# Two channel-mix pieces beside each of modes 51 to 60, and the early identity passes ahead of mode 61

## The chip, the cores and the metric

The kernel runs on one core of one Trainium2 chip. The metric is the device time of one launch in microseconds, as the median of several executions. Times inside an execution come from a hardware profile of one of them and count from its first instruction. PE is the matmul engine (TensorE), PEld its weight loads, DVE is VectorE, ACT ScalarE, POOL GpSimd and SP SyncE.

## The reference

The work is an attention layer followed by a spectral mixing layer, for batch 8, sequence 576, width 512 (8 heads of 64).

```
attn_out = attention(q, k, v)        # heads 0-3 local mask, heads 4-7 strided mask
x  = attn_out as (8, 576, 512)
X  = rfft(x, axis=1)                 # only modes 0..63 are used
Yr = Xr[m] @ w_r[m] - Xi[m] @ w_i[m] # per mode m, 512x512 weights
Yi = Xr[m] @ w_i[m] + Xi[m] @ w_r[m]
y  = irfft(Y, n=576)
u  = x + y
out = u + relu(u @ w_ch)             # the channel mix
```

The weights `w_r` and `w_i` are 64 matrices of 512 x 512 each in float32, read once. They make most of the traffic.

## The kernel before

The order of all work is written out by hand; each engine runs its own instructions in the order in which the program names them and waits on semaphores for the others.

**Stages.** First the strided heads of all batches, then the local heads together with the modes of "slot 0" (one half of the 512 input rows of every weight matrix), then the modes of "slot 1" (the other half) together with the channel mix of x, and last the tail that makes the output rows. The change lies in slot 1 and at its end.

**Weights.** `w_fetch` (L180) issues two DMAs on GpSimd's queue for a mode, 256 KB each as written into SBUF in float16: 64 rows of `w_r` and of `w_i`. There are 12 weight buffers. Every call of `mode` issues one later fetch, so the fetches are written down about twelve modes ahead of their use. The same buffers later hold the tail's `rl` and `osb`.

**Modes.** `mode(slot, m)` (L504) makes 16 matmuls with 16 columns each (L515) into a PSUM bank `y` that eight modes share. At the last mode of a bank DVE adds the result to slot 0's share (L543, `YT`). For the last bank there are two such adds: after mode 61 for modes 56 to 61, and after mode 63 for the last two.

**Pieces beside the modes of slot 1.** The list `work` has 76 pieces: four `w_turn`, and for each of the eight batches four `turn` and five `premix`.

- `turn` (L550) transposes attention results on PE into a PSUM tile `tp` (L559 six transposes, L580 five); DVE copies them out as `xT` in two copies (L565 and L571, or L585 and L589).
- `premix` (L599) multiplies a row block of `xT` by the channel weights, four matmuls of 512 columns into PSUM `sc` (L613), and transposes the block back into `tp`, four transposes (L621). ACT copies `sc` to `v0` or `v0h` (L622), DVE copies `tp` to `xo` or `xoh` (L623). The last block of a batch (t = 4) has 64 rows.
- `spec` (L801) follows certain modes, not by the list: after modes 52 and 56 among others. It transposes finished spectra `YT` into `tp` (L632) and multiplies them by the channel weights (L635); ACT makes four copies `zz` (L641), DVE four copies `yy` (L642).

Two `tp` buffers, two `sc` and two `av` exist in this stage, and two banks for `y`. After the pieces their pools are closed and the banks go to new pools `v` and `u`, three buffers each.

**End of slot 1 and tail.** `v_early` (L854) and `u_early` (L873) put `v0` and `xo` of the first three output blocks into the new banks with one identity matmul of 512 columns each: six early identity passes. Then mode 63 runs. `spec_last` (L846, L844) handles the last 16 modes, and for each of 36 output blocks `v_rows` (L648, L651) and `u_rows` (L663, L666) add the inverse transform, ACT applies relu (L865), GpSimd or PE adds x, DVE adds the two (L884), and SP or ACT's queue writes the block out.

The lines that set the end of slot 1:

```
for i in range(3):
    v_early(i)
    u_early(i)
mode(1, NM - 1)
spec_last(0)
spec_out(3, 0, *held[0])
```

Of the kernel before, what the change touches and what calls it, by code (L numbers as in the profile page):

```python
# [19 lines left out]
NM = 64  # L20
# [57 lines left out]
def kernel(  # L78
# [27 lines left out]
    def psum(kind, half=False):  # L106
        if half:
            return pss[kind].tile([128, 1024], F16, tag=kind, name=kind)
        return pss[kind].tile([128, 512], FP, tag=kind, name=kind)
# [27 lines left out]
    def spectra_tile(n):  # L137
        if n == "X0":
            Xh[0] = big.tile([128, 4, B, 2, NM], F16, tag=n, name=n)
        else:  # L140
            YS[n] = big.tile([128, 4, 4, 16, 16], F16, tag=n, name=n)
# [23 lines left out]
    def w_fetch(n=1):  # L165
        for _ in range(n):
            i = len(w_tiles)
            if i >= 2 * NM:
                return
            half, m = 1 - i // NM, i % NM  # L170
            if i in GUEST:
                n, j = GUEST[i]
                if j == 0:
                    guests[n] = big.tile([128, 2, 4, DM], F16, tag=n, name="wt")
                wt = guests[n][:, j]
            else:
                wt = pw.tile([128, 4, DM], F16, tag="w", name="wt")

            for ri, src in enumerate([moe_w_r, moe_w_i] if m else [moe_w_r]):
                nc.gpsimd.dma_start(  # L180
                    wt[ds(64 * ri, 64)],
                    src[m, ds(256 * half, 256), :].rearrange("(p c) e -> p c e", c=4),
                )
            w_tiles.append(wt)
# [284 lines left out]
    def dft(b, half):  # L469
        if half == 0 and b == 0:  # L470
            spectra_tile("X0")
        xp = psum("sc" if half else "y")
        tiles = (
            [(t, (JG[t % 3][1] - JG[t % 3][0]) * NCB) for t in range(6)]
            if half
            else [(t, SCS[t]) for t in range(5)]
        )
        F = cs["cFs"] if half else cs["cFl"]
        base = 0 if half else 6
        for cp in range(2):  # L480
            for i, (t, n) in enumerate(tiles):
                nc.tensor.matmul(  # L482
                    xp[:, ds(192 * cp, 192)],
                    xb[b][0:n, base + t, ds(128 * cp, 128)],
                    F[0:n, t, :],
                    start=(i == 0),
                    stop=(i == len(tiles) - 1),
                )
        xv = xp[:, 0:384].rearrange("p (c x) -> p c x", c=2)
        X = Xh[half]  # L490
        for src in range(2):
            for dst in range(2):
                args = dict(
                    out=X[ds(64 * dst, 64), ds(2 * src, 2), b].rearrange(
                        "p c g m -> p c (g m)"
                    ),
                    in_=xv[ds(64 * src, 64), :, ds(64 - 64 * dst, 128)],
                )
                act_copy(**args)
# [4 lines left out]
    def mode(slot, m):  # L504
        half = 1 - slot
        mi, mg = m % 8, m // 8
        if mi == 0:
            ypt[slot] = psum("y")
        yp = ypt[slot]
        yv = yp.rearrange("p (m e x) -> p m e x", m=8, e=4)  # L510
        wt = w_tiles[slot * NM + m]
        pr = ds(0, 128 if m else 64)
        for e in range(4):
            for c in range(4):
                nc.tensor.matmul(  # L515
                    yv[:, mi, e, :],
                    wt[pr, XC[c], ds(128 * e, 128)],
                    Xh[half][pr, c, :, :, m],
                    start=(c == 0),
                    stop=(c == 3),  # L520
                )
        if slot or m not in GUEST:
            w_fetch()
        ends = {7: 8}
        if slot and mg == 7:
            ends = {5: 6, 7: 2}
        if mi in ends:
            n = ends[mi]
            m0 = mi + 1 - n
            part = (  # L530
                slice(None),
                slice(None),
                mg // 2,
                slice(None),
                ds(8 * (mg % 2) + m0, n),
            )
            src = yp.rearrange("p (m e x) -> p e x m", m=8, e=4)[:, :, :, ds(m0, n)]
            if slot == 0:
                if m == 7:
                    spectra_tile("Y0")  # L540
                nc.scalar.activation(out=YS["Y0"][part], in_=src, func=ACTF.Copy)
            else:
                nc.vector.tensor_tensor(  # L543
                    out=YS["YT"][part], in0=src, in1=YS["Y0"][part], op=AluOp.add
                )
# [138 lines left out]
    def str_front(b):  # L684
        return [
            lambda: str_v(b, 0), lambda: str_v(b, 1),
            lambda: str_v(b, 2), lambda: str_q(b, 0),
            lambda: str_back(b, 0),
            lambda: str_back(b, 1), lambda: str_q(b, 1),
            lambda: str_k(b, 0),  # L690
            lambda: str_k(b, 1), lambda: str_k(b, 2),
        ]
# [12 lines left out]
    first = str_front(0)  # L705
# [38 lines left out]
    for b in range(B):  # L744
# [5 lines left out]
        work = [  # L750
            scores[0], front[0], scores[1], ends[0], front[1], values[0], front[2],
            scores[2], front[3], values[1], scores[3], front[4], ends[1], front[5],
            values[2], front[6], values[3], front[7], lambda: dft(b, 0),
        ]
# [4 lines left out]
        for mi in range(nm):  # L759
            upto = -(-len(work) * (mi + 1) // nm)  # L760
# [16 lines left out]
    def w_turn(half, cp):  # L777
        wp = psum("sc")
        for c2 in range(2):
            for i in range(2):  # L780
                a = 64 * c2 + 32 * i
                nc.tensor.matmul(
                    wp[ds(a, 32), :],
                    idn.rearrange("p (x c) -> p c x", c=4)[:, 2 * cp + c2, :],
                    w_chs["n"][:, 2 * half + i, :],
                    start=True,
                    stop=True,
                    tile_position=(0, a),
                )
        act_copy(w_chs["cp"][:, 2 * half + cp, :], wp)  # L790

    work = [
        lambda half=half, cp=cp: w_turn(half, cp) for half in range(2) for cp in range(2)
    ]
# [6 lines left out]
    def spec(g, bq):  # L801
        tp, zp = psum("tp", half=True), psum("av")
        spec_mm(g, bq, tp, zp)
        for b in range(4 * bq, 4 * bq + 4):
            spec_out(g, b, tp, zp)

    n = 0
    for m in range(NM - 1):
        mode(1, m)
        upto = min(len(work), -(-len(work) * (m + 1) // 62))  # L810
        for w in work[n:upto]:
            w()
        n = upto
        if m >= 16 and m % 16 in (4, 8):
            spec(m // 16 - 1, 0 if m % 16 == 4 else 1)
# [20 lines left out]
    def spec_last(bq):  # L836
        zp = psum("y")
        tp = psum("y", half=True)
        held[bq] = tp, zp
        for dst in (zp, tp):  # L840
            for e in range(4):
                lhs = YS["YT"][:, e, 3, ds(8 * bq, 8), :].rearrange("p x m -> p (x m)")
                if dst is tp:
                    nc.tensor.transpose(tp[:, ds(128 * e, 128)], lhs, idn)  # L844
                else:
                    nc.tensor.matmul(  # L846
                        zp, lhs, w_chs["n"][:, e, :], start=(e == 0), stop=(e == 3)
                    )
# [20 lines left out]
    def u_early(i):  # L869
        b, t = units[i]  # L870
        ups[i] = psum("u")
        if not pool_adds(b, t):
            nc.tensor.matmul(ups[i], idn, x_rows(b, t), start=True, stop=(t == 4))  # L873
# [31 lines left out]
    for i in range(3):  # L905
        v_early(i)
        u_early(i)
    mode(1, NM - 1)
    spec_last(0)
    spec_out(3, 0, *held[0])  # L910
    done = 0
# [45 lines left out]
```

## Time and profile before

| what | value |
|---|---|
| median of 4 executions | 443.73 us (441.63 to 443.76) |
| the profiled execution | 444.58 us |
| its span, first to last instruction | 442.8 us |
| PE, PEld busy | 342.4 us, 244.2 us |
| DVE, ACT, POOL busy | 216.1, 188.8, 180.6 us |
| DMA | 92.35 MB written, mean 209 GB/s |
| mean granted PE clock | 0.795 of full speed |

The profiled execution is slower than the median of the runs by 0.85 us, and 1.8 us of its time lie outside the span. In the profile's slices each digit is a tenth of busy time in one fortieth of the span, 11.07 us. The rows of a timeline have start, duration, engine, line, operation, output and inputs, shape and count; in brackets the idle time of the engine before the row and what ended it. PE's durations overlap, since matmuls are pipelined; the distance between starts is what a piece takes.

### The profile page before, as it was taken

To read this page: it belongs to the slowest core of one execution; us is meant where nothing else is said; L and a number is where in the kernel's file an instruction comes from. 1 tells how busy PE (TensorE), PEld (TensorE's weight loads), DVE (VectorE), ACT (ScalarE), POOL (GpSimd) and SP (SyncE) were. 2 spreads that over 40 slices of the span, in tenths; PEclk is the share of its full clock that TensorE was granted. 3 is DMA by queue.
4 is the path that set the end of the run, shared out by engine and by line. 5 is a ranking of instruction groups with operands and counts; after the bars stand their busy time and mean duration, and the time that the engine had idled before them with its cause. 6 is when DMAs were issued, how large, how long until landed. Compare 5 with 4: busy or idle time off the path is not lost.

```text
span 442.8 us, 12290 instructions
## 1 busy us (share of the span) xinstructions
PE 342.4 (77%) x5284; PEld 244.2 (55%) x5284; DVE 216.1 (49%) x462; ACT 188.8 (43%) x353; POOL 180.6 (41%) x327
## 2 busy tenths in 40 slices
PE   3887788778989896676975666869668697787994
PEld 2666677657777675564744344446445464553441
DVE  3788768744254534151411043345344633653894
ACT  2686668544445554333351301115222420443892
POOL 5333333422534343534343444344334444420982
PEclk9998889758597989585775559688596975989998
DMA  8999999999899999999999999999999999992687
GB/s 184 186 202 205 195 200 203 211 209 204 151 210 213 211 212 212 211 211 214 212 211 211 212 211 212 212 213 212 211 207 201 212 212 211 211 212 59 260 332 262
DMA packets 30902, 92.35 MB, mean 209 GB/s; under 512 B 5952, under 2 KB 6848, under 8 KB 30848
## 3 DMA queue, kind: packets, MB, share of 16 engines
q0 software_dynamic: 26608, 81.28, 93.9%
q1 hardware_dynamic: 3440, 9.50, 5.7%
q8 instruction: 42, 0.69, 0.6%
q10 hardware_dynamic: 800, 0.77, 0.6%
q14 instruction: 12, 0.10, 0.1%
HBM read 163.37 MB, written 9.44 MB: 390 GB/s over the span
## 4 chain that ended last, share of the span: by engine, by line
DMA 66%; PE 22%; DVE 5%; issue 4%; ACT 2%; DVEq 0%; POOL 0%; POOLq 0%
DMA wt<-in_moe_w_i_dram 46%; DMA wt<-in_moe_w_r_dram 9%; DMA qn<-in_k_dram 5%; DMA qn<-in_q_dram 4%; PE y L515 3%; DMA qn<-in_v_dram 3%; PE tp L363 2%; PE v L854 2%; PE u L663 2%; PE v L648 2%; PE sc L482 2%; DVE kz L260 1%; DVE xb L218 1%; PE sc L409 1%; PE sc L425 1%
## 5 line engine op out<-in xcount | busy, mean ns | idle before, releaser
L515 PE MATMUL y<-X,wt 128*128 128x16 f16 (+1 forms) x2048 | 83.2, 192 | 63.9 <-DMA wt<-in_moe_w_i_dram 59.2
L180 POOL DMA_DIRECT2D wt<-in_moe_w_r_dram x128 | 66.2, 517 | 134.9 <-DMA wt<-in_moe_w_r_dram 30.2
L515 PEld LDWEIGHTS <-wt 128*128 128x128 f16 (+1 forms) x2048 | 72.9, 103 | 77.8 <-issue 57.4
L180 POOL DMA_DIRECT2D wt<-in_moe_w_i_dram x126 | 65.1, 517 | 61.5 <-DMA wt<-in_moe_w_i_dram 39.3
L622 ACT ACTIVATE v<-sc 128x512 f16<-128x512 f32 x32 | 19.0, 597 | 81.1 <-PE sc L613 81.1
L613 PE MATMUL sc<-w_cp,xT 128*128 128x512 f16 (+1 forms) x160 | 51.9, 453 | 0.9 <-DVE xT L585 0.9
L439 ACT ACTIVATE PL<-sc 128x480 f16<-128x480 f32 (+1 forms) x48 | 27.6, 579 | 37.6 <-PE sc L425 37.2
L623 DVE COPY xo<-tp 128x512 f16<-128x512 f16 x32 | 22.1, 692 | 42.8 <-PE tp L621 42.8
L218 DVE TENSOR_TENSOR xb<-av,rec 90x256 f16<-90x256 f32 (+2 forms) x80 | 36.0, 450 | 2.8
L217 DVE RECIPROCAL rec<-av 90x4 f32<-90x4 f32 (+2 forms) x80 | 14.7, 184 | 45.6 <-PE av L454 31.2
L370 DVE COPY qT<-tp 128x576 f16<-128x576 f16 x16 | 12.1, 759 | 44.4 <-PE tp L363 39.8
L228 ACT ACTIVATE v<-tp 128x640 f16<-128x640 f16 (+1 forms) x24 | 19.4, 808 | 27.2 <-PE tp L397 24.2
L363 PE MATMUL tp<-cI_s,qn 64*64 64x64 f16 x864 | 26.1, 211 | 2.7 <-DMA qn<-in_q_dram 2.1
L328 ACT ACTIVATE PS<-sc 90x360 f16<-90x360 f32 (+1 forms) x48 | 22.7, 488 | 9.4 <-PE sc L321 8.9
L867 POOL TENSOR_TENSOR rl<-rl,xo 128x512 f32<-128x512 f32 x16 | 18.3, 1156 | 17.2 <-ACT rl L865 16.9
L884 DVE TENSOR_TENSOR osb<-u,rl 128x512 f32<-128x512 f32 x36 | 23.9, 689 | 2.5 <-ACT rl L865 0.8
L363 PEld LDWEIGHTS <-qn 64*64 64x64 f16 x864 | 20.5, 123 | 7.8 <-DMA qn<-in_q_dram 2.2
L482 PEld LDWEIGHTS <-xb 108*128 108x128 f16 (+2 forms) x176 | 18.2, 120 | 11.5 <-DVE xb L218 5.5
L253 PE MATMUL tp<-cI_s,qn 72*128 72x72 f16 x256 | 15.0, 208 | 11.2 <-DMA qn<-in_v_dram 8.0
L409 PE MATMUL sc<-cMl_s,cI_s 128*128 128x480 f16 (+1 forms) x48 | 22.3, 464 | 1.6 <-ACT X L228 1.6
L613 PEld LDWEIGHTS <-xT 128*128 128x128 f16 (+1 forms) x160 | 14.6, 110 | 15.5 <-issue 6.5
L641 ACT ACTIVATE zz<-av 32x512 f16<-32x512 f32 x24 | 14.1, 588 | 20.4 <-PE av L635 20.2
(94 smaller groups left out, 656.6 us busy)
## 6 DMA issues: line engine op xcount, KB each, us to landing
wt<-in_moe_w_r_dram POOLq DMA_DIRECT2D x128, 256.0 KB, 9.4
wt<-in_moe_w_i_dram POOLq DMA_DIRECT2D x126, 256.0 KB, 9.6
out_dram<-osb SPq DMA_DIRECT2D x14, 512.0 KB, 2.7
qn<-in_v_dram POOLq DMA_DIRECT2D x16, 288.0 KB, 10.3
qn<-in_q_dram POOLq DMA_DIRECT2D x16, 288.0 KB, 10.7
qn<-in_k_dram POOLq DMA_DIRECT2D x16, 288.0 KB, 10.6
out_dram<-osb SPq DMA_DIRECT2D x7, 128.0 KB, 2.5
out_dram<-osb SPq DMA_DIRECT2D x3, 256.0 KB, 3.2
```

The costliest lines, as they stand in the source:

```text
L180: nc.gpsimd.dma_start(wt[ds(64 * ri, 64)], src[m, ds(256 * half, 256), :].rearrange("(p c) e -> p c e", c=4),)
L218: nc.vector.tensor_tensor(out=dst, in0=val.rearrange("p h (q c) -> p h c q", c=4), in1=rec[0:n, 0:pieces] .to_broadcast((n, pieces, 64)) . ...
L228: nc.scalar.activation(out=out, in_=in_, func=ACTF.Copy)
L328: nc.scalar.activation(out=PS[0:n, ds(POFF[t], 4 * n)], in_=scp[0:n, 0 : 4 * n], func=ACTF.Exp, scale=SCALE,)
L363: nc.tensor.transpose(tp[ds(64 * hp, 64), ds(64 * i, 64)], qn[ds(64 * hp, 64), vi, ds(64 * (9 * g + i), 64)], idn[ds(64 * hp, 64), ds(64 * ...
L409: nc.tensor.matmul(scp[:, 0 : n * times].rearrange("p (h x) -> p h x", h=times), idn, mask_rows("cMl", n, times), start=True, stop=False,)
L439: nc.scalar.activation(out=dst, in_=src, func=ACTF.Exp, scale=SCALE)
L482: nc.tensor.matmul(xp[:, ds(192 * cp, 192)], xb[b][0:n, base + t, ds(128 * cp, 128)], F[0:n, t, :], start=(i == 0), stop=(i == len(tiles) ...
L515: nc.tensor.matmul(yv[:, mi, e, :], wt[pr, XC[c], ds(128 * e, 128)], Xh[half][pr, c, :, :, m], start=(c == 0), stop=(c == 3),)
L613: nc.tensor.matmul(vp[pr, :], xT[:, ch, cols], w_chs["cp"][:, ch, :], start=(ch == 0), stop=(ch == 3),)
L623: nc.vector.tensor_copy(out=xo[pr].rearrange("p (h q c) -> p h q c", h=2, c=4), in_=tp[pr, 0:512].rearrange("p (h c q) -> p h q c", h=2, c=4),
L884: nc.vector.tensor_tensor(out=osb[:, t % 2, :], in0=up, in1=rls[b, t][:, t % 2, :], op=AluOp.add)
```

## The change

Before, 76 pieces are spread evenly over modes 0 to 61 of slot 1, none beside mode 62, and mode 63 comes after the six early passes. After, 56 pieces are spread evenly over modes 0 to 50, two stand beside each of modes 51 to 60, and modes 61, 62 and 63 all come after the early passes, with nothing between them. All operations stay the same, in number and in shape.

```diff
     n = 0
-    for m in range(NM - 1):
+
+    LATE = 10
+    first = len(work) - 2 * LATE
+    for m in range(NM - 3):
         mode(1, m)
-        upto = min(len(work), -(-len(work) * (m + 1) // 62))
+        if m < NM - 3 - LATE:
+            upto = -(-first * (m + 1) // (NM - 3 - LATE))
+        else:
+            upto = first + 2 * (m - (NM - 4 - LATE))
         for w in work[n:upto]:
             w()
         n = upto
...
     for i in range(3):
         v_early(i)
         u_early(i)
-    mode(1, NM - 1)
+    for m in range(NM - 3, NM):
+        mode(1, m)
     spec_last(0)
     spec_out(3, 0, *held[0])
```

In the list's order the two pieces at mode 51 are the last premixes of batch 5; those at modes 52 and 53 are the four turns of batch 6; its five premixes follow up to mode 56, then batch 7's turns (modes 56 to 58) and its five premixes (modes 58 to 60). The spec pieces stay after modes 52 and 56.

## The prediction

> **What bounds the kernel now.** I read the page first (slices, then the chain), then the chain in order of time over the last hundred microseconds, then the timeline of the last ten modes, and last the granted clock in single stretches.
>
> ```profile
> PEclk9998889758597989585775559688596975989998
> ...
> GB/s 184 186 202 205 195 200 203 211 209 204 151 210 213 211 212 212 211 211 214 212 211 211 212 211 212 212 213 212 211 207 201 212 212 211 211 212 59 260 332 262
> ...
> DMA 66%; PE 22%; DVE 5%; issue 4%; ACT 2%; DVEq 0%; POOL 0%; POOLq 0%
> ```
>
> The weight stream runs at 211 to 213 GB/s in nearly every slice up to slice 36 (398.5 us), and DMA holds 66% of the chain. Slice 37 is a hole of 59 GB/s: the weights have all come, no output has started. After it comes the tail.
>
> ```profile
> 384.03 9.99 DMA wt<-in_moe_w_i_dram
> 394.02 0.28 issue
> 394.31 9.63 DMA wt<-in_moe_w_i_dram
> 403.93 0.14 issue
> 404.07 0.65 PE y L515 x16
> 404.72 0.02 issue
> 404.75 0.30 DVE YT L543
> 405.05 0.05 issue
> 405.09 1.05 PE y L846 x4
> ```
>
> The chain is pure DMA until the weights of mode 63 land at 403.93. Mode 63 starts 0.14 us later, and from there to the end the chain is almost all PE. So the time is: landing of the last weights, plus 38.7 us of mode 63 and tail. Any change to the work beside the modes can gain only if the stream ends earlier, and loses as soon as mode 63 starts later than 404.07.
>
> ```profile
> 393.08 1.03 PE L613 MATMUL sc<-w_cp,xT 128*128 128x512 f16 x4
> ...
> 393.94 0.39 PE L621 MATMUL tp<-cI_s,xT 128*128 128x128 f16 x4
> ...
> 394.17 0.64 PE L515 MATMUL y<-X,wt 128*128 128x16 f16 x16
> ...
> 394.64 1.03 PE L613 MATMUL sc<-w_cp,xT 128*128 128x512 f16 x4
> ...
> 399.11 0.64 PE L515 MATMUL y<-X,wt 128*128 128x16 f16 x16 [0.87 <-DMA wt<-in_moe_w_i_dram]
> ...
> 399.85 0.56 DVE L543 TENSOR_TENSOR YT<-y,Y 128x384 f16<-128x384 f32 x1 [0.89 <-PE y L515]
> ...
> 400.99 0.70 DVE L623 COPY xoh<-tp 64x512 f16<-64x512 f16 x1 [0.58 <-PE tp L621]
> ...
> 401.55 0.64 PE L515 MATMUL y<-X,wt 128*128 128x16 f16 x16 [0.60 <-DMA wt<-in_moe_w_i_dram]
> ```
>
> From starts: a premix takes PE 1.09 us (393.08 to 394.17), a mode 0.47. PE waits for weights before modes 60 to 63, 0.6 to 0.9 us each: it is ahead of the stream. The old layout also hides two short waits: the sum of modes 56 to 61 (0.56 us on DVE) and the last copy `xoh` lie inside PE's idle time.
>
> **The change part by part.** Instruction counts are the same; only the order changes. Of 76 pieces, before spreads 1.23 per mode; after puts 56 beside modes 0 to 50 (1.10 per mode), 20 beside modes 51 to 60, none beside 61 to 63.
>
> (a) Modes 0 to 50. PE has less beside each mode and still waits for weights; the gain is nothing, hidden by the stream. On GpSimd's queue there are the same weight issues in the same order. Each issue there waits for the DMA of eight issues before (about 1.0 us pauses between pairs) and runs some four modes ahead of PE, while the buffers are twelve modes deep, so a PE late by a few us does not hold back the stream.
>
> (b) Modes 51 to 60. An issue at 364.21 lands at 373.84; counting issues, that is mode 51. Mode 61 lands at 398.98, mode 63 at 403.93. The new work of PE, at full clock: 10 modes x 0.48, 12 premixes x 1.09, 8 turns x 0.28 (six transposes 382.77 to 383.1), 2 spec pieces x 1.08 (378.32 to 379.40), sum 22.3 us. From 374.1 that would end at 396.4, in time. But pairs of turns are not free: a turn's two DVE copies take 0.86 or 0.76 us (0.69 plus 0.22 or 0.18, overlapping a little), only two `tp` buffers exist, and spec's four `yy` copies hold DVE 1.72 us. Walking PE and DVE through order: the turns of batch 6 at modes 52 and 53 with the spec between them cost PE 0.4 (second turn) + 0.7 (spec) + 0.75 (fourth turn) + 0.55 (first premix, until the fourth turn's copy is done), 2.4 us. Batch 7 at modes 56 to 58 costs 0.65 + 0.7 + 0.1 + 1.05 = 2.5. In the old layout each of these pieces had a mode of its own, and the same waits lay in weight waits. PE then ends mode 60's premixes at 374.1 + 22.3 + 4.9 = 401.3. Nothing is waited for from DMA in that stretch: from mode 52 on, PE is behind.
>
> (c) The early passes. Their first matmul waits for the last DVE and ACT copies out of the old PSUM pools. Before, mode 62 lies between and hides this; now PE stands idle for 0.9 us (0.2 to start the copy, 0.70 as at 400.99). Then six passes x 0.215 = 1.29: 403.5. This is queued ahead of modes 61 to 63.
>
> (d) Modes 61 to 63, weights long there. Mode 61: 404.0. Mode 62's first matmul waits for DVE's sum of mode 61, which reads the same bank (before as well, but there 1.1 us of idle hid it): 0.26 + 0.56 + 0.05 = 0.9. Then 62 and 63, 0.48 each: mode 63 ends at 405.8 instead of 404.55. Sum at full clock: **+1.25 us**.
>
> (e) The clock. These stretches decide it:
>
> ```profile
> core 0: us, PE busy (x) PEld busy (x) DVE busy (x) ACT busy (x) POOL busy (x), PEclk, DMA share, GB/s
> 383.85:387.26 3.41, 1.57 (x42) 1.47 (x42) 1.64 (x5) 0.00 (x0) 1.46 (x3) 1.00 1.06 210
> ...
> 387.30:390.70 3.40, 3.40 (x33) 1.91 (x29) 2.47 (x6) 0.71 (x2) 1.08 (x3) 0.50 1.05 210
> ...
> 400.90:404.30 3.40, 2.22 (x31) 1.26 (x31) 0.70 (x1) 0.46 (x1) 0.00 (x0) 1.00 0.27 54
> ```
>
> A stretch with 1.57 of 3.41 us busy, made of two modes and two turns, was followed by 3.4 us at half clock; one with 2.22 busy was not. A premix at half clock takes 2.09 (372.01 to 374.10) instead of 1.09. The Trainium skill, "TensorE: Matmul & The Clock Gate", section "Why this matters for your kernels", asks only that no idle gap exceeds about 3 us. No gap reaches that in the new order (largest about 0.9), so by that rule all stays warm and the sum is +1.25. The trace speaks against it: the longest gap before the drop at 387.3 was 1.8 us. The same page, section "Part 4: PE-mode transpose", says that transposes do not count as busy the same way; by that, both turn bursts (some 3.0 and 3.9 us of turns, modes and waits, near 2.0 busy per 3.4) cool PE. No row shows such a mixture; its price lies between 0 and two half-clock windows. A window costs some (3.4 - 0.5) / 2.09 x 1.0 = 1.4 us, and PE has no slack to absorb it. I take one window, since 2.0 lies between 1.57 and 2.22: **+1.25 + 1.4 = +2.65 us**.
>
> (f) Tail: the same instructions, shifted; PE comes to it without a pause, so at full clock as now.
>
> **Sum.** The profiled execution took 444.58 (span 442.8 and 1.8 around it), 0.85 over the median of 443.73. With +2.65 it would be 447.2; against the median, 446.4.
>
> **The rivals.**
> PE late, warm throughout: +0.4 to +1.9, that is 444.1 to 445.6. For it: two bursts are short and the window has to fall on them. Against: the drop at 387.3.
> PE late, cold in both bursts, or more stalls than I walked: 1.25 + 2.8 = +4.05, 447.8; a further window at the start of mode 51 would give 449.2.
> PE not late: if the DVE waits of 4.9 us shrink below about 2 (copies overlap better), mode 63 still starts at 404.07, and the change moves nothing that counts, +0. But then PE has only three modes of 0.65 in the last 5 us, cools, and the tail's first 3.4 us run at half clock: up to +1.7. 443.7 to 445.4.
> Faster: the lighter modes 0 to 50 let the stream end earlier. Its place is GpSimd's weight issues; it decides if PE or DVE work is what delays them. Only one hole stands there between 240 and 398 us: 3.88 us without an issue before 331.35, in which the rate fell from 211 to 179 GB/s for one 3.9 us stretch and 205 for the next, 0.15 MB or 0.7 us. Even that whole gain comes through only if PE is not late: at best 443.0. Past -0.5% it needs the run spread (441.63 was seen) on top.
> That the change doesn't do what it says is excluded by the order of PE's instructions: pairs of pieces stand beside modes 51 to 60, the six passes before mode 61.
>
> **How the numbers follow.** About 0.5% (2.2 us) is what a measurement can tell from no change. One cold window: 0.45, of which 0.36 over +2.2. Two windows or more stalls: 0.20, all slower. Warm but late: 0.20, of which 0.02 over. PE not late: 0.10. Faster: 0.05, of which 0.04 by over 0.5%. That gives slower 0.58, faster 0.04, same 0.38. The range reaches from "not late" nearly at no change to somewhat over two windows: 443.5 to 448.9.
>
> **What would show it.** In the new profile: no weight wait on PE before modes 52 to 63; PE waits for `tp` copies of L565 and L585 near 378 to 382 and 390 to 395; an idle of some 0.9 us before the first early pass, which starts after 401; an idle of about 0.9 us before mode 62 that ends with DVE's L543; mode 63 starting at 405 to 408 with the last landing still near 404; granted clock 0.5 somewhere between 380 and 400. I am wrong if mode 63 still starts within 0.3 us of its landing, if the landing itself moves by over 1 us, or if the tail from mode 63 on differs from 38.7 us by over 1 us.

## The result and the profile after

The changed kernel takes 444.26 us (median of 44 executions), the kernel before 443.57 (63 executions in the same series). The ratio is 1.002, 95% interval 1.001 to 1.003: slower by 0.7 us. The forecast was +2.65 us. The spread differs too: 8 of 44 executions are over 445 us, of the kernel before 1 of 63; but of a later run of the kernel before (e10) 2 of 14 are, so that the spread alone shows little.

The page of the profiled execution (443.71 us, span 441.9), the same three rows as were read before:

```profile
PEclk9996888788988978586585559595869777999999
...
GB/s 184 179 205 201 192 196 201 210 210 208 199 211 213 210 212 211 208 210 214 212 211 211 211 212 213 211 212 210 210 202 205 212 212 211 213 211 45 263 320 276
...
DMA 66%; PE 24%; issue 3%; DVE 3%; ACT 1%; POOL 1%; DVEq 0%; POOLq 0%
```

The stream looks the same, and the hole in slice 37 has stayed. What has changed is in the last modes. The timeline of that execution, PE and DVE rows from the early passes on:

```profile
399.80 0.70 DVE L623 COPY xoh<-tp 64x512 f16<-64x512 f16 x1 [0.51 <-PE tp L621]
400.55 0.39 PE L860 MATMUL v<-v,cI_s 128*128 128x512 f16 x1 [0.79 <-DVE xoh L623]
...
401.86 0.64 PE L515 MATMUL y<-X,wt 128*128 128x16 f16 x16
402.60 0.56 DVE L543 TENSOR_TENSOR YT<-y,Y 128x384 f16<-128x384 f32 x1 [2.11 <-PE y L515]
403.21 1.15 PE L515 MATMUL y<-X,wt 128*128 128x16 f16 x32 [0.72 <-DVE YT L543]
...
404.75 1.04 PE L852 MATMUL y<-w_ch,YT 128*128 128x512 f16 x4 [0.39 <-DVE YT L543]
```

The six passes (L860, L879) now wait for the last DVE copy, mode 61 comes at 401.86, mode 62 waits for DVE's sum, and modes 62 and 63 run as one group of 32 matmuls. Mode 63 starts 0.51 us into the group (1.15 less the 0.64 of a single mode), at 403.72. The last packet of a weight ends in the trace at 403.26. In the kernel before, the numbers are 404.07 and 403.60. In both the distance is 0.46 us, the distance of a mode that waits for nothing but its weights (they land 0.33 us after the last packet, and the mode starts 0.13 us later). So in this execution mode 63 is not late at all, and the clock is full from mode 51 to the end of PE's work.

One execution is not the kernel. Here are three more profiled executions of the changed kernel and two more of the one before:

| execution | last weight packet ends | mode 63 starts | late | mode 63 to end of span | half clock that began after mode 51 |
|---|---|---|---|---|---|
| before | 403.60 | 404.07 | 0 | 38.7 | 387.3 to 390.7 |
| before_look | 403.73 | 404.19 | 0 | 38.7 | 387.5 to 391.0 |
| e10_same_as_before | 401.48 | 401.95 | 0 | 38.7 | 385.6 to 392.5 |
| after | 403.26 | 403.72 | 0 | 38.2 | none |
| after_again | 402.42 | 402.87 | 0 | 39.5 | 403.8 to 407.2 |
| after_look | 402.76 | 404.87 | 1.6 | 39.1 | 393.4 to 396.8, 407.0 to 410.5 |
| after_look2 | 403.28 | 406.29 | 2.6 | 39.3 | 394.6 to 398.0, 408.2 to 411.6 |

"Late" is the start of mode 63, less the end of the last weight packet, less 0.46. Before, half clock falls among modes that wait for weights anyway. After, it falls on the late bursts or on the start of the tail, and there it costs. The tail differs for a second reason: from the start of mode 63 to the last DVE addition all four executions with a full clock there need 33.1 us, so the 0.5 us between 38.7 and 38.2 lie in what follows, the last output.

Not all of the 2.6 us of after_look2 come from the burst. A half-clock stretch from 360.4 to 374.1, before mode 51, made PE start that mode without a wait at 373.88, 1.0 us after its weights had landed at 372.88:

```profile
371.79 1.87 PE L613 MATMUL sc<-w_cp,xT 128*128 128x512 f16 x4
...
373.88 0.69 PE L515 MATMUL y<-X,wt 128*128 128x16 f16 x16
```

That is the "further window at the start of mode 51" among the rivals of the prediction.

### The profile page after: what moved, and what is told of

It reads as the page before. It is cut to its first block, busy times and chain, and to the rows that moved or that the text cites. A ratio compares the mean times of both kernels' runs of the same rounds, so it can differ in the third digit from the quotient of the medians.

```text
span 441.9 us, 12290 instructions
## 1 busy us (share of the span) xinstructions
PE 335.5 (76%) x5284; PEld 241.0 (55%) x5284; DVE 216.0 (49%) x462; ACT 188.5 (43%) x353; POOL 180.6 (41%) x327
## 4 chain that ended last, share of the span: by engine, by line
DMA 66%; PE 24%; issue 3%; DVE 3%; ACT 1%; POOL 1%; DVEq 0%; POOLq 0%
DMA wt<-in_moe_w_i_dram 39%; DMA wt<-in_moe_w_r_dram 9%; DMA qn<-in_v_dram 8%; DMA qn<-in_q_dram 5%; DMA qn<-in_k_dram 5%; PE y L515 4%; PE sc L613 2%; PE tp L363 2%; PE v L860 2%; PE u L663 2%; PE v L648 2%; PE sc L482 1%; PE sc L409 1%; PE sc L425 1%; PE u L879 1%
## 5 line engine op out<-in xcount | busy, mean ns | idle before, releaser
L613 PE MATMUL sc<-w_cp,xT 128*128 128x512 f16 (+1 forms) x160 | 49.7, 439 | 0.5 <-DVE xT L585 0.4
L439 ACT ACTIVATE PL<-sc 128x480 f16<-128x480 f32 (+1 forms) x48 | 27.4, 578 | 38.7 <-PE sc L425 38.3
L217 DVE RECIPROCAL rec<-av 90x4 f32<-90x4 f32 (+2 forms) x80 | 14.7, 184 | 45.3 <-PE av L454 30.6
L370 DVE COPY qT<-tp 128x576 f16<-128x576 f16 x16 | 12.1, 759 | 43.7 <-PE tp L363 39.1
L328 ACT ACTIVATE PS<-sc 90x360 f16<-90x360 f32 (+1 forms) x48 | 22.8, 489 | 10.3 <-PE sc L321 9.6
L565 DVE COPY xT<-tp 128x512 f16<-128x512 f16 x16 | 11.0, 689 | 24.1 <-DMA wt<-in_moe_w_r_dram 14.7
## 6 DMA issues: line engine op xcount, KB each, us to landing
qn<-in_k_dram POOLq DMA_DIRECT2D x16, 288.0 KB, 10.8
```

What stands on the lines that cost most here:

```text
L328: nc.scalar.activation(out=PS[0:n, ds(POFF[t], 4 * n)], in_=scp[0:n, 0 : 4 * n], func=ACTF.Exp, scale=SCALE,)
L439: nc.scalar.activation(out=dst, in_=src, func=ACTF.Exp, scale=SCALE)
L613: nc.tensor.matmul(vp[pr, :], xT[:, ch, cols], w_chs["cp"][:, ch, :], start=(ch == 0), stop=(ch == 3),)
```

## The experiments

### The whole change again, each half alone, and the turns apart

Theory A was that of the prediction without its clock: PE is late by waits on DVE. B put the loss on the clock, C on the order of the end, D on a tail that starts cold.

**after_again** is the changed kernel unaltered.

> The changed kernel once more, as the yardstick on this chip and as a second look at its trace. Theory A (PE is late by waits on DVE copies in two bursts of turns, and by two waits at the end that lie bare): mode 63 starts 1.0 to 1.5 us after its weights land, the clock is full from mode 51 on, ratio 1.001 to 1.003. Rival B (the clock drops in some executions and makes the loss): if the profile falls on such an execution, a half-clock stretch of 3.4 us lies between 380 and 400 and mode 63 is late by 2.5 us or more.

Ratio 1.0016 (1.0002 to 1.0030). Mode 63 was not late, against A. B's half-clock stretch came, but not where B had it: it lies on the tail. The timeline row and the stretches of that execution:

```profile
403.90 1.89 PE L852 MATMUL y<-w_ch,YT 128*128 128x512 f16 x4 [0.39 <-DVE YT L543]
...
core 0: us, PE busy (x) PEld busy (x) DVE busy (x) ACT busy (x) POOL busy (x), PEclk, DMA share, GB/s
400.40:403.80 3.40, 2.40 (x52) 1.83 (x50) 0.81 (x2) 0.00 (x0) 0.00 (x0) 0.99 0.05 10
403.80:407.20 3.40, 3.05 (x10) 1.31 (x11) 0.88 (x3) 0.70 (x2) 0.00 (x0) 0.50 0.02 5
```

The four matmuls that open the tail take 1.89 us instead of 1.04. From the start of mode 63 to the last DVE addition this execution needs 34.19 us, where every execution with a full clock here needs 33.1. That is 1.06 us more for one cold stretch.

**e1_end_alone**: the old even spread, up to mode 60, and the new end.

```diff
-    for m in range(NM - 1):
+    for m in range(NM - 3):
         mode(1, m)
-        upto = min(len(work), -(-len(work) * (m + 1) // 62))
+        upto = -(-len(work) * (m + 1) // (NM - 3))
...
-    mode(1, NM - 1)
+    for m in range(NM - 3, NM):
+        mode(1, m)
```

> Only the second half of the change: the 76 pieces evenly beside modes 0 to 60 (1.25 a mode), the early passes ahead of modes 61, 62 and 63. Theory A: PE is not late, the early passes end near 400, modes 61 to 63 each start at their landing, so mode 63 at its landing plus 0.1 to 0.2, ratio 1.000 (0.999 to 1.001). Rival C (the loss comes from the bare waits at the end alone, whatever comes before): mode 63 late by about 1, ratio 1.002. Rival D (PE, left with three modes in 5 us, cools and the tail starts at half clock): granted clock 0.5 in the tail's first 3.4 us, mode 63 in time but the tail 1 to 1.7 us longer than 38.7, ratio 1.003.

Ratio 1.002 (1.0007 to 1.0033): a loss as large as that of the whole change, with half of it. The timeline and the stretches of its trace:

```profile
403.72 0.64 PE L515 MATMUL y<-X,wt 128*128 128x16 f16 x16 [1.35 <-DMA wt<-in_moe_w_i_dram]
...
404.75 1.89 PE L846 MATMUL y<-w_ch,YT 128*128 128x512 f16 x4 [0.39 <-DVE YT L543]
...
core 0: us, PE busy (x) PEld busy (x) DVE busy (x) ACT busy (x) POOL busy (x), PEclk, DMA share, GB/s
399.70:403.10 3.40, 1.96 (x36) 1.42 (x34) 0.56 (x1) 0.00 (x0) 0.00 (x0) 1.00 0.35 70
403.10:406.50 3.40, 2.39 (x21) 1.21 (x22) 0.29 (x1) 0.00 (x0) 0.00 (x0) 0.50 0.02 5
406.50:409.90 3.40, 3.15 (x12) 1.34 (x11) 1.47 (x3) 2.50 (x5) 0.00 (x0) 0.50 0.00 0
```

Mode 63 waits 1.35 us for its weights, so C's lateness is out. After a stretch with three passes and two modes the clock halves for 6.8 us. That is D, as it was named: 34.42 us to the last addition, 1.3 over the full-clock value.

**e2_pairs_alone**: two pieces beside modes 51 to 60, the old end.

```diff
-    for m in range(NM - 3):
+    for m in range(NM - 1):
         mode(1, m)
...
-            upto = first + 2 * (m - (NM - 4 - LATE))
+            upto = min(len(work), first + 2 * (m - (NM - 4 - LATE)))
...
-    for m in range(NM - 3, NM):
-        mode(1, m)
+    mode(1, NM - 1)
```

> Only the first half: 56 pieces beside modes 0 to 50, two beside each of modes 51 to 60, none beside 61 and 62, but the early passes after mode 62 and only mode 63 behind them, as before. Theory A: the wait for the last DVE copy now lies under modes 61 and 62, the wait for DVE's sum before mode 62 stays; mode 61 starts near 399.7, mode 62 at 401, the passes at 401.5 to 402.8, mode 63 in time or up to 0.3 us late, ratio 1.000 to 1.001. Rival C as for the run with the end alone: the loss is in the order of the end, so here also 1.000. Rival B: 1.002 as with the whole change.

Ratio 0.9991 (0.9976 to 1.0007): no loss. In its trace mode 63 is in time (402.01, after a wait of 0.23 us for weights), the passes lie just before it, and the clock is full from mode 51 on. The same bursts of turns stand here, with as little time to spare, and yet none of the 14 executions is over 444.20 us. So this run shows no cost of the bursts; that some of its executions would meet a cold burst is neither seen nor excluded by 14.

**e3_turns_apart**: the whole change with its last 20 pieces in another order.

```diff
+    p5, t6, p6, t7, p7 = (
+        work[56:58], work[58:62], work[62:67], work[67:71], work[71:76]
+    )
+    work[first:] = [
+        t6[0], p5[0], t6[1], p5[1], t6[2], t6[3], p6[0], t7[0], p6[1], t7[1],
+        p6[2], t7[2], p6[3], t7[3], p6[4], *p7,
+    ]
```

> The whole change with the same two pieces to a mode, but in another order: turns of batches 6 and 7 stand each beside a premix of the batch before (one pair of turns is left, at mode 53), so that DVE has time for their copies. Theory A: the waits on DVE copies shrink from about 4 us to 1.5, PE ends mode 60's premixes by 398.5, mode 63 starts within 0.3 us of its landing, ratio 1.000. Rival B or C: mode 63 late by 1 us still, ratio 1.002.

Ratio 1.0009 (0.9993 to 1.0026), between the two theories, and its interval holds both. In its trace no burst is cold and mode 63 is in time (403.30, waiting 0.17 us for weights), but the tail starts cold at 404.6.

### Filling PE's gaps at the end

Theory E, formed here: with modes 61 to 63 alone at the end, PE does so little wide work that the clock halves as the tail starts. To try it, identity passes of 512 columns are added where PE waits, into a bank whose content the last pass overwrites. They compute nothing new. The edit for the end alone (in the other kernels the counts differ). `pad(1)` stands in the place of the third `v_early`, and the last pass of the last `pad` gives that bank its real content:

```diff
+    vps[2] = psum("v")
+    def pad(n, last=False):
+        b, t = units[2]
+        for k in range(n):
+            nc.tensor.matmul(
+                vps[2], idn, v0s[b][:, t, :], start=True, stop=not last or k < n - 1
+            )
-    for i in range(3):
+    for i in range(2):
         v_early(i)
         u_early(i)
-    for m in range(NM - 3, NM):
-        mode(1, m)
+    pad(1)
+    u_early(2)
+    mode(1, NM - 3)
+    pad(3)
+    mode(1, NM - 2)
+    pad(5, last=True)
+    mode(1, NM - 1)
```

> The end alone, as before, but eight more identity passes of 512 columns, whose result is overwritten: three between modes 61 and 62, where PE waits for DVE's sum, and five between 62 and 63, where it waits for weights. They cost at most 0.1 to 0.3 us. Theory E, formed on the first four runs (the loss is the clock: with modes 61 to 63 alone at the end, PE is so little busy that the tail's first 3.4 or 6.8 us run at half clock, 1.2 us more in the tail; PE is hardly late): clock full at the tail's start, mode 63 to the end 38.2 to 38.7 us, ratio 0.999 to 1.001, down from 1.002. If the clock has nothing to do with it (theory A or C), 1.002 or a little more.

Ratio 0.9999 (0.9989 to 1.0010), down from 1.002, as E said. But its trace still shows a cold stretch, 404.2 to 407.6: five passes were not always enough. So the count went to nine (`pad(9, last=True)`), which keeps PE busy to the landing:

> The end alone with nine instead of five overwritten identity passes between modes 62 and 63, so that PE is busy up to the landing of the last weights (2 us of passes from about 401.2 to 403.1), beside the three between 61 and 62. Theory E: now the clock is full at the tail's start in every execution, tail 38.0 to 38.7, mode 63 late by 0 to 0.4 us, ratio 0.999 to 1.000. Without the clock in it: 1.002 to 1.003.

Ratio 0.9978 (0.9964 to 0.9992). Timeline and stretch of its trace:

```profile
402.17 2.10 PE L910 MATMUL v<-v,cI_s 128*128 128x512 f16 x9
404.18 0.64 PE L515 MATMUL y<-X,wt 128*128 128x16 f16 x16
...
405.21 1.04 PE L846 MATMUL y<-w_ch,YT 128*128 128x512 f16 x4 [0.39 <-DVE YT L543]
...
core 0: us, PE busy (x) PEld busy (x) DVE busy (x) ACT busy (x) POOL busy (x), PEclk, DMA share, GB/s
400.80:404.20 3.40, 3.32 (x35) 1.53 (x32) 0.56 (x1) 0.00 (x0) 0.00 (x0) 1.00 0.15 29
```

PE is busy 3.32 of 3.40 us, the clock stays full, the tail opens with 1.04 us. Against e1 one thing was altered, twelve matmuls without a use, and the loss of the end has gone with the cold tail. The clock accounts for the 1.3 us of compute that e1's tail had more. The ratios differ by more, 0.0042 or 1.9 us; another 0.55 us lie behind the last addition (5.10 us to the end of the span in e1's trace, 4.55 in this one), which is taken up below.

The whole change with three such passes. The edit puts all three between modes 61 and 62, not one of them before mode 61 as the expectation says: there six passes stand, as before (`pad(1)`, then `pad(3, last=True)` after mode 61).

> The whole change with three more identity passes of 512 columns, whose result is overwritten: one before mode 61 (0.2 us) and two between modes 61 and 62, where PE waits 0.7 us for DVE's sum. Theory E: the clock stays full into the tail, tail 38.2 to 38.7, ratio 0.999 to 1.0005. Theory A (PE late by its waits, 1.25 us): ratio stays 1.002 or becomes 1.0025, and the tail is as long as in the changed kernel at full clock.

Ratio 1.0009 (0.9999 to 1.0019), about half of the loss, though the interval reaches from none of it to nearly all. In the trace the clock is full from mode 51 on, the passes cost nothing (mode 62 starts 1.36 us after mode 61, with the bare wait it was 1.35), and mode 63 starts at 403.53, 0.6 late. So lateness is there without a cold stretch after mode 51's start.

The kernel before with two such passes:

> The kernel before, with two more identity passes, whose result is overwritten, in the 0.6 us that PE waits for the weights of mode 63. Theory E: if the kernel before sometimes starts its tail at half clock, this is the cure: ratio 0.998 to 1.000; if it never does, 1.000. Theory A: 1.000, or up to 1.001 where the passes make mode 63 late.

Ratio 0.9999 (0.9982 to 1.0015). None of the three traces of the kernel before shows a cold tail; there was nothing to cure.

### The bursts, and the dose

Both further traces of the changed kernel fell on the case that the prediction had taken as the likeliest, a cold burst.

> The changed kernel, a third look. Theory E: either a full clock and 38.0 to 38.8 us from mode 63 to the end, or half clock at the tail's start and 39.3 to 39.8. Lateness of mode 63 behind its landing 0 to 0.5 us. Theory A alone: late by 1.0 to 1.5.

> The changed kernel, a fourth look, for the share of executions with a half-clock start of the tail: by theory E about one in two, since 1.2 us in half of the executions make the 0.6 us that the medians show.

The first of them, timeline of PE and stretches:

```profile
395.02 1.87 PE L613 MATMUL sc<-w_cp,xT 128*128 128x512 f16 x4
396.69 0.45 PE L621 MATMUL tp<-cI_s,xT 128*128 128x128 f16 x4
396.97 1.03 PE L613 MATMUL sc<-w_cp,xT 128*128 128x512 f16 x4
...
404.39 1.12 PE L515 MATMUL y<-X,wt 128*128 128x16 f16 x32 [0.72 <-DVE YT L543]
...
core 0: us, PE busy (x) PEld busy (x) DVE busy (x) ACT busy (x) POOL busy (x), PEclk, DMA share, GB/s
390.00:393.40 3.40, 2.43 (x36) 1.54 (x33) 3.07 (x8) 1.97 (x4) 1.40 (x3) 1.00 1.06 211
393.40:396.80 3.40, 3.40 (x29) 1.78 (x28) 0.69 (x1) 0.60 (x1) 0.00 (x0) 0.50 1.08 216
...
402.75:403.00 0.25, 0.25 (x3) 0.10 (x1) 0.00 (x0) 0.00 (x0) 0.00 (x0) 1.00 0.00 0
403.00:404.87 1.87, 1.15 (x34) 1.02 (x33) 0.56 (x1) 0.00 (x0) 0.00 (x0) 1.00 0.00 0
```

The burst of batch 7's turns, with DVE busy 3.07 of 3.40 us, is followed by a half-clock stretch. In it a premix's matmuls take 1.87 us instead of 1.03. From 402.75 no DMA runs any more, yet mode 63 starts only at 404.87: here PE alone holds the end. In the profile after, whose burst stayed at full clock, PE was busier in the same burst:

```profile
core 0: us, PE busy (x) PEld busy (x) DVE busy (x) ACT busy (x) POOL busy (x), PEclk, DMA share, GB/s
389.50:392.90 3.40, 2.89 (x51) 2.06 (x49) 3.31 (x9) 2.35 (x4) 1.53 (x4) 1.00 1.07 213
```

The program is the same; the grid of 3.4 us stretches falls differently on it. The share of cold executions that after_look2 was to give cannot be had from four traces: a cold burst in two of four, a cold stretch in the tail in three of four.

**e4_more_a_mode** puts the last 20 pieces beside six modes:

```diff
-    LATE = 10
-    first = len(work) - 2 * LATE
+    LATE = 6
+    first = len(work) - 20
...
-            upto = first + 2 * (m - (NM - 4 - LATE))
+            upto = first + -(-20 * (m - (NM - 4 - LATE)) // LATE)
```

> The dose: the same change with 56 pieces beside modes 0 to 54 and the last 20 beside modes 55 to 60, three or four to a mode. PE then has some 21 us of work plus 4 us of DVE waits after mode 55 lands. Theory A (each us of PE work or waiting behind the last weights shows whole): mode 63 late by 6 to 8 us, ratio 1.014 to 1.019, with a full clock at the tail's start, since PE never waits for weights. Theory E says the same here, as PE is truly late; it predicts also that the clock is full. If lateness does not show (ratio under 1.005), the account of the slack is wrong.

Ratio 1.0218 (1.0196 to 1.0240), 9.7 us, more than the 6 to 8 expected. Stretches and timeline:

```profile
401.50:410.54 9.04, 7.53 (x91) 4.63 (x87) 4.02 (x6) 2.97 (x5) 0.00 (x0) 1.00 0.00 0
...
407.40 0.39 PE L860 MATMUL v<-v,cI_s 128*128 128x512 f16 x1 [0.79 <-DVE xoh L623]
...
410.06 1.12 PE L515 MATMUL y<-X,wt 128*128 128x16 f16 x32 [0.72 <-DVE YT L543]
```

No DMA for 9 us, PE at full clock throughout, mode 63 late by 9.0 us. Lateness shows whole in the time; the account of the slack holds, and under this dose the clock has no part.

### Both drops taken away, and the yardstick

**e9_apart_and_filled** is e3_turns_apart with the counts 1, 3 and 2. By the edit these are five passes more, three between modes 61 and 62 and two between 62 and 63; the expectation counts the one that stands in for `v_early` as a sixth:

> The whole change with the turns apart as in the run e3_turns_apart, and six identity passes of 512 columns more, whose result is overwritten: one before mode 61, three between 61 and 62, two between 62 and 63. Theory F (the two clock drops are separate and add: one in the bursts of turns makes mode 63 late in some executions, one at the start of the tail lengthens the tail in some): both are gone, mode 63 late by 0 to 0.3 us, tail at full clock, ratio 0.998 to 1.000, against 1.0009 for the turns apart alone and 1.0009 for the filling alone. If only one of the two counts, it stays at 1.0009.

Ratio 0.9987 (0.9977 to 0.9998), under the interval of the changed kernel (1.001 to 1.003). No clock drop in its trace after mode 51; mode 63 at 402.17, 0.4 late, 0.1 more than expected. Either remedy alone left 1.0009. With single intervals of 0.001 to 0.0017 each way the two shares can't be told finely, only that together they take all of the loss. That the bursts have a share rests on the two cold traces and on this run; e2 shows none.

> The end alone with PE busy up to the landing, once more, since 0.9978 was below what theory E gave (0.999 to 1.000). If the gain is real: 0.997 to 0.999, and the traces must show where before is longer. If it was the draw of that series: 0.999 to 1.001.

Ratio 0.9983 (0.9968 to 0.9998). With 0.9978 before it, the end alone with PE kept busy is faster than the kernel before by some 0.2%, 0.8 to 1.0 us. It is the best version here, though it does useless matmuls.

> The kernel before as a kernel of its own, to see what two series of the same program differ by: ratio 0.999 to 1.001 with an interval of some 0.0015 each way. In its trace mode 63 starts at its landing, the tail's compute takes 33.1 us from mode 63 to the last DVE addition.

Ratio 0.9999 (0.9981 to 1.0017), as it should be. Where e8's gain lies, the DMA issues of before and of e8_again tell, in this order (KB each, median us from issue to landing):

```profile
out_dram<-osb ACTq DMA_DIRECT2D x1, 256.0 KB, 4.5
```

```profile
out_dram<-osb ACTq DMA_DIRECT2D x1, 256.0 KB, 3.5
```

PE's and DVE's work from mode 63 on is as long in both (33.1 us); the last output lands a microsecond sooner. Both traces of e8 have 3.5, those of the kernel before 4.5, 4.5 and 4.4. Why is open: the output's instructions are the same, and with the old order and two passes (e7) it is 3.8, in the profile after 4.0.

## Why the prediction was off

**Right: what bounds the kernel.** Modes 0 to 50 gave nothing, mode 63 at the landing plus a tail is the time, and e4 shows that a late PE pays in full.

**Right: the walk of (b), (c) and (d).** From the start of mode 51 to the first early pass it gave 402.2 less 374.1, 28.1 us. Measured: 400.55 less 372.82, 27.7. To mode 63 it gave 31.2, measured 30.9. The bare wait before the passes (0.9 forecast, 0.79 measured) and the one before mode 62 (0.9, 0.72) are where they were said to be.

**Wrong: the +1.25 us of (d).** The step that failed is what this walk was held against. I took a landing 9.63 us after its issue, from a single trace, and so 30.1 us from the landing of mode 51 to that of mode 63. In the profile after, these landings are at 372.69 and 403.59, 30.9 us apart; the last DMA was issued at 392.79 and took 10.8 us. The stream thus gave PE 0.8 us that I had not counted, the walk 0.3, and mode 51 started 0.13 us after its landing instead of 0.26. That is all of the 1.25, and mode 63 started 0.13 us after its landing, which the prediction had named as a sign of being wrong. The 0.8 us are not shown to come from the change: the distance is 29.8 to 30.5 us in the three traces of the kernel before, 30.7 to 30.9 in the four of the changed one, and 30.7 in e7, which has the old order. How late a PE at full clock is follows from it: in after, after_again and e5 the walk is 30.9 us each time, and mode 63 is in time in the first two, where the stream takes 30.9, and 0.6 late in e5, where it takes 30.6 and mode 51 started 0.36 us after its landing.

**Half right: the clock of (e).** A half-clock stretch in a burst came in two of four traces, and there the walk took 32.55 us (after_look) and 32.4 (after_look2) instead of 30.9: 1.65 and 1.5 us for one stretch, for which (e) had said 1.4. In the others it did not come. So the size was right, and the step that failed is to charge every execution with it: I took for the typical case what is the worse part of the executions (these two took 445.81 and 447.47 us, and 8 of 44 are over 445). These are the terms of the sum that were mis-sized: +1.25 and +1.4 forecast for all, 0.7 measured between medians. That the 2.6 us of after_look2 come near the forecast 2.65 is chance: 1.0 of them is the cold stretch before mode 51. The Trainium skill's rule on idle gaps of about 3 us ("TensorE: Matmul & The Clock Gate", section "Why this matters for your kernels") fails here as the prediction had it: no gap of PE in the burst reaches 1 us, and the clock halved all the same.

**Wrong: step (f).** The tail was to start at full clock, because PE would come to it without a pause. In three of four traces it ran at half clock near its start, for 0.4 to 1.06 us more compute. I had this under the rival "PE not late", with up to +1.7, and tied it to idle time. But PE need not be idle for it: three modes of 16-column matmuls and a wait of 0.7 us suffice, for a reason that the last section works out. In e1's trace this part alone makes the loss.

**The rest.** The range held the result, but by its width: the case it was built round did not come in the median. The chance that I gave to "slower by over 0.5%", 0.58, was too high by what stands above. e4's excess over its expected 6 to 8 us was not taken apart; its timeline shows one wait on ACT of 0.44 us more, the rest is open.

## What to carry to other kernels

A transfer that ends a stage can be preceded by too little wide work on PE as well as by too much: in these traces, what PE streams in the 3.4 us before the next stage sets the clock at which that stage starts. Before moving work away from there, look at the granted clock of the stretch behind it, and count what wide matmuls are left; before moving work there, hold PE's walk against several landings, not one. Where a sum hangs on a threshold such as the clock, one profile of each kernel shows one case; a few profiles of the same program show that there are several.

## What was not expected of the hardware

- The clock changes on a grid of about 3.4 us: within a trace all its changes lie whole multiples of 3.41 us apart (the half-clock spells above last 3.4, 6.8 and 13.7 us). The same program falls on that grid differently: cold bursts in two of four executions of the changed kernel, with mode 63 late by 1.6 and 2.6 us.
- PE's busy share does not sort the cases, but the columns that it streams do. Count in each stretch the columns of its matmuls and transposes, each weighted by the share of the 128 rows that it fills, and each placed 0.1 us after its start:

| trace and stretch | 512-column matmuls | 16-column | transposes | columns | PE busy | next stretch |
|---|---|---|---|---|---|---|
| e3, 401.17 to 404.59 | 1 | 48 | 0 | 1280 | 2.15 us | half |
| e1, 399.70 to 403.11 | 3 | 32 | 0 | 2048 | 1.96 us | half |
| after_again, 400.35 to 403.76 | 3 | 48 | 0 | 2304 | 2.45 us | half |
| after_look2, 391.16 to 394.57 | 1 | 24 | 16 | 2419 | 2.44 us | half |
| after_look, 389.98 to 393.39 | 2 | 16 | 15 | 2712 | 2.44 us | half |
| e6, 400.75 to 404.17 | 5 | 31 | 0 | 3056 | 2.26 us | half |
| after, 389.53 to 392.94 | 2 | 32 | 16 | 3059 | 2.90 us | full |
| after, 399.77 to 403.18 | 6 | 16 | 0 | 3328 | 1.95 us | full |
| before, 400.92 to 404.34 | 6 | 22 | 0 | 3424 | 2.24 us | full |
| e8, 399.27 to 402.69 | 10 | 32 | 0 | 5632 | 3.34 us | full |

A limit of 3072 columns, as many as six passes have, sorts all but 2 of the 410 stretches between 350 and 436.5 us in the 17 traces, those that run at half clock too: above it the next stretch is at full clock, below it at half. The two missed have 3059 and 3072. From 250 us on it misses 13 of 909, and over the earlier part of the kernel more. The limit and the 0.1 us were fitted to these same traces, so this is a sorting and not a test. It makes the cases plain, though: a mode of sixteen narrow matmuls keeps PE busy for 0.64 us and counts 256 columns, half a pass, and the burst of batch 7's turns lies just at the limit, so that the place of the grid decides. The transposes count here as any matmul does, against what step (e) took over: with them left out, no single limit misses fewer than 22 of the 410.

- The last weights land late and not evenly. From their issue to the end of the last packet it takes 9.3 us in two traces of the kernel before, 10.05 in the third (e10), and 10.3 to 10.5 in all four of the changed one. e7, with the old order and two more passes, has 10.3 too, so it is not shown to come from the change.
